# Ordering an mLSTM and mixture-of-depths kernel by hand on one core, with a narrower state product and gates by pairs

## The chip, the cores and the metric

The kernel runs on one core of a Trainium2 chip. The time is the device time of one execution in microseconds (us); the median of several runs is given. The engines are TensorE (PE in the profile; PEld is its loading of weights), VectorE (DVE), ScalarE (ACT), GpSimd (POOL) and SyncE (SP), which only issues transfers here. Each engine works through its own list of instructions in order and waits on semaphores for the others.

## The reference, cut to what matters

There are two blocks. The first is an mLSTM cell over 4 batch rows, 8 heads, 768 tokens and a head size of 40; the second treats its output, 320 wide, as tokens of which the 128 highest scored in each batch row pass a small two-layer network.

```python
for t in range(S):                                   # S = 768, per batch row and head
    m_new  = np.maximum(f_gate[:, :, t] + m, i_gate[:, :, t])
    f_stab = np.exp(f_gate[:, :, t] + m - m_new)
    i_stab = np.exp(i_gate[:, :, t] - m_new)
    m = m_new
    C = f_stab[..., None, None] * C + i_stab[..., None, None] * np.einsum('bhd,bhe->bhde', vt, kt)
    n = f_stab[..., None] * n + i_stab[..., None] * kt
    h_tilde = np.einsum('bhde,bhe->bhd', C, qt)
    denom = np.maximum(np.abs(np.einsum('bhd,bhd->bh', n, qt)[..., None]), 1.0)
    y[:, :, t] = sigmoid(o_gate[:, :, t]) * h_tilde / denom
x = y laid out as (B, S, 320)
scores = np.einsum('bsd,d->bs', x, w_gate)
for b in range(B):
    top = np.argpartition(-scores[b], 128)[:128]
    ye = np.maximum(x[b, top] @ w1, 0.0) @ w2        # 320 -> 1024 -> 320
    out[b, top] = x[b, top] + sigmoid(scores[b, top])[:, None] * ye
```

## The kernel before

The recurrence is done in chunks of 128 tokens: 4 batch rows of 6 chunks are 24 steps. Within a chunk the gates become a matrix W of weights between two tokens, and the state C of all heads is carried from chunk to chunk. One column of ones beside v carries n along with C, so a head has 41 columns, padded to 64 in the state and in the banks of PSUM. All data are 32-bit floats but for the operands of W.

Before a step, a chunk is prepared: W from two small matmuls (pW), an exponential and a causal mask, v scaled by the gates (wv), and k and q transposed (pt to T).

```python
    def prepare(b, c, qk, v1, so):
        W = work.tile([128, H, L], FP, name="W")
        for h0 in range(0, H, 4):
            rows_in = slice(64 * (b % 2) + 8 * h0, 64 * (b % 2) + 8 * h0 + 32)
            pW = ps_t.tile([128, 4, L], FP, name="pW", tag="t")
            nc.tensor.matmul(pW, a_o[b // 2, c][rows_in], M_o[b // 2, c][rows_in], start=True, stop=True)
            nc.scalar.activation(out=W[:, h0:h0 + 4, :], in_=pW, func=AF.Exp)
        nc.gpsimd.affine_select(out=W, in_=W, compare_op=OP.is_ge, fill=0.0, base=0, pattern=[[0, H], [1, L]],
                                channel_multiplier=-1)
        wv = None
        if c < NT - 1:
            wv = work.tile([128, H, D1], FP, name="wv")
            nc.gpsimd.tensor_tensor(out=wv, in0=v1[:, :, 0:D1], op=OP.mult,
                                    in1=cols[c][:, 0, b * H:(b + 1) * H].unsqueeze(2).to_broadcast([128, H, D1]))
        T = work.tile([128, 2, NP, L], FP, name="T")
        for j in range(2):
            pt = ps_t.tile([128, NP, L], FP, name="pt", tag="t")
            for p in range(NP):
                nc.tensor.transpose(pt[:, p, :], qk[:, j, 2 * p:2 * p + 2, :].rearrange("s a d -> s (a d)"), ident)
            nc.scalar.copy(out=T[:, j], in_=pt)
        nc.scalar.activation(out=so, in_=so, func=AF.Tanh, scale=0.5)
        nc.scalar.add(so, so, 1.0)
        return W, T, wv
```

A step then forms the products of q and k (pS), weighs them (P), reads the old state (pI), updates it (pC), adds the part within the chunk (pH) and divides. x is the finished chunk, and its product with w_gate (the reduction into sc) is its score.

```python
    def mlstm_chunk(b, c, qk, v1, so, W, T, wv, x, sc):
        hs = slice(b * H, (b + 1) * H)
        k_n = qk[:, 0]
        P = work.tile([128, NP, 2, L], FP, name="P", bufs=2)
        pS = [ps_s.tile([128, NP, L], FP, name="pS") for _ in range(2)]
        for p in range(NP):
            for j in range(2):
                e = HALVES[j]
                nc.tensor.matmul(pS[j][:, p, :], T[e, 0, p, :], T[e, 1, p, :], start=True, stop=True)
        for j in range(2):
            nc.vector.tensor_tensor(out=P[:, :, j, :], in0=pS[j], op=OP.mult,
                                    in1=W.rearrange("p (n a) t -> p n a t", a=2)[:, :, j, :])
        C = C_t[(b * NT + c) % 3]
        num = None
        if c > 0:
            pI = ps_a.tile([128, H, DP], FP, name="pI", tag="a")
            for p in range(NP):
                for t in HALVES:
                    nc.tensor.matmul(pI[t, 2 * p:2 * p + 2, :].rearrange("t a d -> t (a d)"), T[:, 1, p, t],
                                     C[:, p].rearrange("e a d -> e (a d)"), start=True, stop=True)
            num = work.tile([128, H, D1], FP, name="num")
            nc.vector.tensor_tensor(out=num, in0=pI[:, :, 0:D1], op=OP.mult,
                                    in1=cols[c][:, 1, hs].unsqueeze(2).to_broadcast([128, H, D1]))
        if c < NT - 1:
            pC = ps_a.tile([128, NP, D1], FP, name="pC", tag="a")
            for p in range(NP):
                for j, e in enumerate(HALVES):
                    nc.tensor.matmul(pC[e, p, :], k_n[:, 2 * p + j, :], wv[:, 2 * p + j, :], start=True, stop=True)
            Cn = C_t[(b * NT + c + 1) % 3]
            if c > 0:
                nc.gpsimd.tensor_tensor(out=Cn[:, :, :, 0:D1], in0=C[:, :, :, 0:D1], op=OP.mult,
                                        in1=cols[c][:, 2, hs].rearrange("p (n a) -> p n a", a=2).unsqueeze(3)
                                        .to_broadcast([128, NP, 2, D1]))
            for j in range(2):
                e = slice(j * DP, j * DP + D)
                Cj, pj = Cn[e, :, j, 0:D1], pC[e]
                if c == 0:
                    nc.vector.tensor_copy(out=Cj, in_=pj)
                else:
                    nc.vector.tensor_tensor(out=Cj, in0=Cj, in1=pj, op=OP.add)
        pH = ps_a.tile([128, H, DP], FP, name="pH", tag="a")
        for h in range(H):
            for t in HALVES:
                nc.tensor.matmul(pH[t, h, :], P[:, h // 2, h % 2, t], v1[:, h, :], start=True, stop=True)
        if num is None:
            num = pH
        else:
            nc.vector.tensor_tensor(out=num, in0=num, in1=pH[:, :, 0:D1], op=OP.add)
        den = work.tile([128, H], FP, name="den")
        nc.vector.tensor_scalar(out=den, in0=num[:, :, D], scalar1=-2.0, scalar2=2.0, op0=OP.mult, op1=OP.max)
        nc.vector.scalar_tensor_tensor(out=den, in0=num[:, :, D], scalar=2.0, in1=den, op0=OP.mult, op1=OP.max)
        rec = work.tile([128, H], FP, name="rec")
        nc.vector.reciprocal(out=rec, in_=den)
        sor = work.tile([128, H, D], FP, name="sor")
        nc.gpsimd.tensor_tensor(out=sor, in0=so, in1=rec.unsqueeze(2).to_broadcast([128, H, D]), op=OP.mult)
        nc.vector.tensor_tensor(out=x[:, c, :].rearrange("p (h d) -> p h d", d=D), in0=num[:, :, 0:D], in1=sor,
                                op=OP.mult)
        scr = work.tile([128, DM], FP, name="scr", bufs=1)
        nc.vector.tensor_tensor_reduce(out=scr, in0=x[:, c, :], in1=wg, scale=1.0, scalar=0.0,
                                       op0=OP.mult, op1=OP.add, accum_out=sc[:, c:c + 1])
        nc.gpsimd.dma_start(out=out[b, c * L:(c + 1) * L, :], in_=x[:, c, :])
```

The gates are computed for several chunks at once, in the groups 0, 1 to 2 and 3 to 5. They lie on 128 partitions, four copies of the 32 pairs of batch row and head, so that the three bfloat16 parts of a number (split) can be multiplied in one matmul (operands: a_o and M_o, from which pW is made).

```python
    def gates(c0, c1):
        g, n = slice(c0, c1), c1 - c0
        nc.vector.tensor_tensor_scan(out=flat(F[:, g]), data0=flat(again[:, g]), data1=flat(f_sb[:, g]), initial=0.0,
                                     op0=OP.mult, op1=OP.add)
        nc.vector.tensor_tensor(out=a[:, g], in0=i_sb[:, g], in1=F[:, g], op=OP.subtract)
        nc.vector.tensor_tensor_scan(out=flat(Mg[:, g]), data0=flat(low[:, g]), data1=flat(a[:, g]), initial=0.0,
                                     op0=OP.add, op1=OP.max)
        nc.vector.tensor_tensor_scan(out=m[:, c0 + 1:c1 + 1], data0=Mg[:, g, L - 1], data1=F[:, g, L - 1],
                                     initial=m[:, c0:c0 + 1], op0=OP.max, op1=OP.add)
        mb = m[:, g].unsqueeze(2).to_broadcast([128, n, L])
        nc.vector.tensor_tensor(out=Mg[:, g], in0=Mg[:, g], in1=mb, op=OP.max)
        nc.vector.tensor_tensor(out=wk[:, g], in0=a[0:BH, g], in1=Mg[0:BH, g, L - 1:L].to_broadcast([BH, n, L]),
                                op=OP.subtract)
        nc.scalar.activation(out=wk[:, g], in_=wk[:, g], func=AF.Exp)
        nc.vector.tensor_tensor(out=r[:, g], in0=mb[0:BH], in1=Mg[0:BH, g], op=OP.subtract)
        nc.scalar.activation(out=r[:, g], in_=r[:, g], func=AF.Exp)
        split(M3, Mg, g)
        split(a3, a, g)
        for c in range(c0, c1):
            operands(0, c)
            pc = ps_m.tile([128, 3, BH], FP, name="pc", tag="m")
            for j, row in enumerate((wk[:, c, :], r[:, c, :], r[:, c, L - 1:L].to_broadcast([BH, L]))):
                nc.tensor.transpose(pc[:, j, :], row, ident[0:BH, 0:BH])
            cols.append(const.tile([128, 3, BH], FP, name=f"cols{c}"))
            nc.vector.tensor_copy(out=cols[c], in_=pc)
```

The order of the program is this; a scheduler decides from it how the instructions stand on each engine. The second block's parts are compare (pb spreads a chunk's scores over the partitions, ge and cnt count larger ones), ranks (pcol, sel), gather (pidx, and a transfer of the chosen rows into xe), enter (pX, xeT, the sigmoid), layer1 (ph) and layer2 (py, and a transfer back).

```python
    for n, (b, c) in enumerate(steps):
        for ahead in range(1, AHEAD + 1):
            load(n + ahead)
        if n == 1:
            gates(3, NT)
        if n == 4:
            load_weights()
        if NT <= n < 2 * NT and B > 2:
            operands(1, n - NT)
        if c == NT // 2 and b + 1 < B:
            state[b + 1] = open_batch(b + 1)
        prepared(n + 1)
        mlstm_chunk(b, c, *ready[n], *state[b][0])
        if n > 0:
            compare(*steps[n - 1], *state[steps[n - 1][0]][1])
        if b > 0:
            if c == 1:
                todo = ranks(b - 1, *state[b - 1][1][2:])
            elif c == 2:
                todo = gather(b - 1, todo)
            elif c == 3:
                todo = enter(todo)
                layer1(todo, 0)
            elif c == 4:
                layer1(todo, 1)
            elif c == 5 and b < B - 1:
                layer2(b - 1, todo)
    compare(*steps[-1], *state[B - 1][1])
    picked = gather(B - 1, ranks(B - 1, *state[B - 1][1][2:]))
    if B > 1:
        layer2(B - 2, todo)
    picked = enter(picked)
    for half in range(2):
        layer1(picked, half)
    layer2(B - 1, picked)
```

## Time and profile before

| what | value |
|---|---|
| median of 3 runs | 248.35 us (247.83 to 256.67) |
| span of the profiled run | 250.0 us |
| mean TensorE clock granted in it | 0.914 of full speed |
| transfers | 24.94 MB, 102860 packets, of which 100688 under 512 B |
| queue of the loads (q1) | 16.13 MB, 42.4% of 16 engines' span |
| queue of GpSimd (q0) | 8.03 MB, 10.0% |

A row of the profile's groups gives the line, engine, operation and tiles, the count, the busy time and the mean of one in ns, and the idle time of the engine before it with what ended that. A row of the timeline gives start and duration in us, engine, line, operation, output and inputs, and in brackets the idle time before it. In the rows of 40 slices each digit is a tenth of a slice of 6.25 us; a 9 in the row PEclk stands for 0.9 or more of full speed. Ends of matmuls are modelled, so the distance between starts is the better measure of what a group of matmuls takes.

### The profile page before, as it was taken

To read this page: it belongs to the slowest core of one execution; us is meant where nothing else is said; L and a number is where in the kernel's file an instruction comes from. 1 tells how busy PE (TensorE), PEld (TensorE's weight loads), DVE (VectorE), ACT (ScalarE), POOL (GpSimd) and SP (SyncE) were. 2 spreads that over 40 slices of the span, in tenths; PEclk is the share of its full clock that TensorE was granted. 3 is DMA by queue.
4 is the path that set the end of the run, shared out by engine and by line. 5 is a ranking of instruction groups with operands and counts; after the bars stand their busy time and mean duration, and the time that the engine had idled before them with its cause. 6 is when DMAs were issued, how large, how long until landed. Compare 5 with 4: busy or idle time off the path is not lost. (4 is left out here: it accounts for less than half of the span.)

```text
span 250.0 us, 6255 instructions
## 1 busy us (share of the span) xinstructions
PE 202.1 (81%) x2474; PEld 162.7 (65%) x2474; DVE 166.1 (66%) x450; ACT 89.9 (36%) x199; POOL 110.4 (44%) x148
## 2 busy tenths in 40 slices
PE   0175399999788998699999986999999859927890
PEld 0164268778566786589768774987687749915780
DVE  6479986387888798948637888555478795763100
ACT  1243372255345555332544552523534322100010
POOL 4185651256543757532257575332575633221101
PEclk9998555579999999889999999999999999995998
DMA  4999999539864766573346666563250110000000
GB/s 80 180 156 193 216 283 141 65 61 179 156 116 83 136 124 119 120 131 55 81 105 108 126 116 141 111 113 62 79 108 4 42 41 29 26 29 26 26 0 26
DMA packets 102860, 24.94 MB, mean 100 GB/s; under 512 B 100688, under 2 KB 100944, under 8 KB 102832
## 3 DMA queue, kind: packets, MB, share of 16 engines
q1 hardware_dynamic: 100224, 16.13, 42.4%
q0 software_dynamic: 2224, 8.03, 10.0%
q10 hardware_dynamic: 384, 0.39, 0.8%
q8 instruction: 19, 0.31, 0.5%
q14 instruction: 9, 0.07, 0.1%
HBM read 19.96 MB, written 4.59 MB: 98 GB/s over the span
## 5 line engine op out<-in xcount | busy, mean ns | idle before, releaser
L250 PE MATMUL pS<-T 64*128 64x128 f32 x384 | 40.6, 311 | 0.1
L252 DVE TENSOR_TENSOR P<-pS,W 128x512 f32<-128x512 f32 x48 | 31.4, 681 | 12.8 <-PE pS L250 12.7
L250 PEld LDWEIGHTS pS<-T 64*128 64x128 f32 x384 | 31.5, 202 | 9.4 <-issue 7.2
L289 PE MATMUL pH<-v,P 128*64 128x64 f32 x768 | 31.5, 234 | 6.3 <-DVE P L252 3.1
L221 ACT ACTIVATE W<-pW 128x512 f32<-128x512 f32 x48 | 26.9, 596 | 24.8 <-PE pW L220 24.5
L222 POOL TENSOR_SCALAR_AFFINE_SELECT W<-W 128x1024 f32<-128x1024 f32 x24 | 28.2, 1175 | 17.1 <-ACT W L221 16.9
L289 PEld LDWEIGHTS pH<-v,P 128*64 128x64 f32 x768 | 27.0, 145 | 12.4 <-DVE num L264 6.1
L233 PE MATMUL pt<-ident,qk 128*128 128x128 f32 x192 | 32.4, 312 | 3.0 <-ACT W L221 2.7
L302 POOL TENSOR_TENSOR sor<-so,rec 128x320 f32<-128x320 f32 x24 | 17.6, 731 | 32.0 <-DVE rec L300 31.9
L234 ACT COPY T<-pt 128x512 f32<-128x512 f32 x48 | 26.6, 587 | 11.7 <-PE pt L233 11.5
L233 PEld LDWEIGHTS pt<-ident,qk 128*128 128x128 f32 x192 | 24.1, 158 | 7.5 <-ACT W L221 4.8
L227 POOL TENSOR_TENSOR wv<-v,cols 128x328 f32<-128x328 f32 x20 | 15.3, 763 | 31.2 <-PE pC L272 8.5
L386 PE MATMUL ph<-xeT,w 128*128 128x128 f32 x192 | 23.8, 279 | 0.8 <-DVE xeT L375 0.8
L261 PE MATMUL pI<-C,T 128*64 128x128 f32 x320 | 24.3, 290 | 0.0
L386 PEld LDWEIGHTS ph<-xeT,w 128*128 128x128 f32 x192 | 22.3, 192 | 1.6 <-DVE xeT L375 1.0
L316 ACT COPY sb<-pb 128x128 f32<-128x128 f32 x24 | 6.4, 266 | 45.9 <-PE pb L315 45.9
L308 POOL DMA_DIRECT2D out_dram<-x x24 | 14.1, 589 | 18.1 <-DVE x L303 16.5
L303 DVE TENSOR_TENSOR x<-num,sor 128x320 f32<-128x320 f32 x20 | 9.8, 492 | 18.4 <-POOL sor L302 18.4
L275 POOL TENSOR_TENSOR C<-C,cols 128x328 f32<-128x328 f32 x16 | 16.1, 1008 | 12.5 <-DVE C L284 10.4
L394 PE MATMUL py<-w,hT 128*128 128x320 f32 x64 | 20.6, 475 | 0.0
L261 PEld LDWEIGHTS pI<-C,T 128*64 128x64 f32 x320 | 18.6, 142 | 2.9 <-issue 0.6
L318 DVE SCALAR_TENSOR_TENSOR ge<-sb,sc,earlier 128x128 bf16<-128x128 f32 (+5 forms) x24 | 16.9, 704 | 1.9 <-ACT sb L316 1.3
(107 smaller groups left out, 275.7 us busy)
## 6 DMA issues: line engine op xcount, KB each, us to landing
qk<-in_k_dram SPq DMA_DIRECT2D x24, 160.0 KB, 3.5
qk<-in_q_dram SPq DMA_DIRECT2D x24, 160.0 KB, 3.7
v<-in_v_dram SPq DMA_DIRECT2D x24, 160.0 KB, 3.0
so<-in_o_gate_dram SPq DMA_DIRECT2D x24, 160.0 KB, 2.9
out_dram<-x POOLq DMA_DIRECT2D x24, 160.0 KB, 2.6
w<-in_moe_w_dram POOLq DMA_DIRECT2D x1, 1280.0 KB, 7.9
w<-in_moe_w_dram POOLq DMA_DIRECT2D x2, 512.0 KB, 8.1
i_sb<-in_i_gate_dram ACTq DMA_DIRECT2D x4, 80.0 KB, 6.1
```

Source lines behind the costliest of these rows:

```text
L221: nc.scalar.activation(out=W[:, h0:h0 + 4, :], in_=pW, func=AF.Exp)
L222: nc.gpsimd.affine_select(out=W, in_=W, compare_op=OP.is_ge, fill=0.0, base=0, pattern=[[0, H], [1, L]], channel_multiplier=-1)
L233: nc.tensor.transpose(pt[:, p, :], qk[:, j, 2 * p:2 * p + 2, :].rearrange("s a d -> s (a d)"), ident)
L234: nc.scalar.copy(out=T[:, j], in_=pt)
L250: nc.tensor.matmul(pS[j][:, p, :], T[e, 0, p, :], T[e, 1, p, :], start=True, stop=True)
L252: nc.vector.tensor_tensor(out=P[:, :, j, :], in0=pS[j], op=OP.mult, in1=W.rearrange("p (n a) t -> p n a t", a=2)[:, :, j, :])
L261: nc.tensor.matmul(pI[t, 2 * p:2 * p + 2, :].rearrange("t a d -> t (a d)"), T[:, 1, p, t], C[:, p].rearrange("e a d -> e (a d)"), start=Tr ...
L289: nc.tensor.matmul(pH[t, h, :], P[:, h // 2, h % 2, t], v1[:, h, :], start=True, stop=True)
L302: nc.gpsimd.tensor_tensor(out=sor, in0=so, in1=rec.unsqueeze(2).to_broadcast([128, H, D]), op=OP.mult)
L318: nc.vector.scalar_tensor_tensor(out=ge[:, GE[u]:GE[u + 1]], in0=sb.rearrange("p t l -> p (t l)")[:, 0:n], scalar=sc[:, u:u + 1], in1=earl ...
L386: nc.tensor.matmul(ph[:, f, :], w1[:, j, (f0 + f) * 128:(f0 + f + 1) * 128], xeT[:, j, :], start=(j == 0), stop=(j == NDC - 1))
L394: nc.tensor.matmul(py, hT[:, f, :], w2[:, f, :], start=(f == 0), stop=(f == NFC - 1))
```

## The change

The scheduler is switched off and the order on every engine is written by hand, step by step. Each of the following goes with it.

- T, W and wv are made two steps ahead; pb and the comparison take the scores of the step before; ph and py are spread over the steps in pieces, and in the last stretch py stands between the comparison and the gather.
- pI and pC share one bank of PSUM (pIC) and are not padded: the state has 41 columns a head, so pI streams 82 columns for two heads instead of 128.
- The causal mask is applied to each half of W as soon as its exponential is done.
- The stores of x and the loads of w1, w2 and w_gate are issued by SP, the loads' queue, instead of GpSimd.
- The gates are computed in the groups 0, 1, 2 to 3 and 4 to 5, on 32 partitions. The three parts of a number are now three tiles, and the operands come from six accumulated matmuls instead of two; the two exponentials of the gates are done chunk by chunk with the subtraction as their bias. Parts of the splitting go to ACT and GpSimd.
- Four chunks instead of three are loaded ahead.

The diff, cut to its core:

```diff
-    C_t = [const.tile([128, NP, 2, DP], FP, name=f"C{n}") for n in range(3)]
+    C_t = [const.tile([128, NP, 2, D1], FP, name=f"C{n}") for n in range(3)]
...
+        for x, xs, cast, sub in zip((Mg, a), parts, (nc.scalar.copy, nc.gpsimd.tensor_copy), (nc.vector, nc.gpsimd)):
+            if c0 == 0:
+                cast, sub = nc.vector.tensor_copy, nc.vector
+            rest = gate.tile([BH, 2, L], FP, name="rest", bufs=2)
+            cast(out=xs[0][:, g], in_=x[:, g])
+            sub.tensor_tensor(out=rest[:, 0:n], in0=x[:, g], in1=xs[0][:, g], op=OP.subtract)
+            cast(out=xs[1][:, g], in_=rest[:, 0:n])
+            sub.tensor_tensor(out=xs[2][:, g], in0=rest[:, 0:n], in1=xs[1][:, g], op=OP.subtract)
+    def scales(c):
+        nc.scalar.activation(out=wk[:, c], in_=a[:, c], func=AF.Exp, bias=nM[:, c:c + 1], scale=1.0)
+        nc.scalar.activation(out=r[:, c], in_=Mg[:, c], func=AF.Exp, bias=m[:, c:c + 1], scale=-1.0)
...
+        pO = ps_m.tile([128, 2, L], FP, name="pO", tag="m")
+        for j in range(2):
+            for part in range(3):
+                nc.tensor.matmul(pO[:, j, :], place[j][u][:, part].rearrange("p g k h -> p (g k h)"),
+                                 parts[j][part][:, c, :], start=(part == 0), stop=(part == 2))
+        M_o[u, c] = const.tile([128, 4, L], BF, name=f"M_o{u}{c}")
+        a_o[u, c] = const.tile([128, L], BF, name=f"a_o{u}{c}")
+        nc.scalar.activation(out=a_o[u, c], in_=pO[:, 1, :], func=AF.Identity, bias=of[:, 0:1], scale=1.0)
+        nc.vector.scalar_tensor_tensor(out=M_o[u, c], in0=pO[:, 0, :].unsqueeze(1).to_broadcast([128, 4, L]),
+                                       scalar=of[:, 1:2], in1=which.unsqueeze(2).to_broadcast([128, 4, L]),
+                                       op0=OP.add, op1=OP.mult)
...
-        nc.gpsimd.dma_start(out=w2, in_=moe_w2.rearrange("(f p) d -> p f d", p=128))
...
+            nc.sync.dma_start(out=w1[0:w, j, :], in_=moe_w1[d0:d0 + w, :])
+        nc.sync.dma_start(out=w2, in_=moe_w2.rearrange("(f p) d -> p f d", p=128))
...
-        nc.gpsimd.affine_select(out=W, in_=W, compare_op=OP.is_ge, fill=0.0, base=0, pattern=[[0, H], [1, L]],
-                                channel_multiplier=-1)
...
+            nc.gpsimd.affine_select(out=W[:, h0:h0 + 4, :], in_=W[:, h0:h0 + 4, :], compare_op=OP.is_ge, fill=0.0, base=0,
+                                    pattern=[[0, 4], [1, L]], channel_multiplier=-1)
...
+    def exchange(b, c, qk, T, wv):
+        pIC = ps_c.tile([128, (H + NP) * D1], FP, name="pIC")
+        pI, pC = pIC[:, 0:H * D1], pIC[:, H * D1:].rearrange("p (n d) -> p n d", d=D1)
+        if c > 0:
+            C = C_t[(b * NT + c) % 3]
+            for p in range(NP):
+                for t in HALVES:
+                    nc.tensor.matmul(pI[t, 2 * p * D1:2 * (p + 1) * D1], T[:, 1, p, t],
+                                     C[:, p].rearrange("e a d -> e (a d)"), start=True, stop=True)
...
-            pI = ps_a.tile([128, H, DP], FP, name="pI", tag="a")
-            for p in range(NP):
-                for t in HALVES:
-                    nc.tensor.matmul(pI[t, 2 * p:2 * p + 2, :].rearrange("t a d -> t (a d)"), T[:, 1, p, t],
-                                     C[:, p].rearrange("e a d -> e (a d)"), start=True, stop=True)
...
-        pH = ps_a.tile([128, H, DP], FP, name="pH", tag="a")
-        for h in range(H):
-            for t in HALVES:
-                nc.tensor.matmul(pH[t, h, :], P[:, h // 2, h % 2, t], v1[:, h, :], start=True, stop=True)
...
+        pH = ps_h.tile([128, H, DP], FP, name="pH")
+        for j in range(2):
+            for p in range(NP):
+                for t in HALVES:
+                    nc.tensor.matmul(pH[t, 2 * p + j, :], P[:, p, j, t], v1[:, 2 * p + j, :], start=True, stop=True)
...
+        nc.sync.dma_start(out=out[b, c * L:(c + 1) * L, :], in_=x)
...
-        nc.gpsimd.dma_start(out=out[b, c * L:(c + 1) * L, :], in_=x[:, c, :])
...
+    def weighed(n):
+        W[n] = weigh(*steps[n])
+        wv[n] = scaled_v(*steps[n], loaded[n][1])
+    def first_weighed(n):
+        c = steps[n][1]
+        operands(0, c)
+        W[n] = weigh(*steps[n])
+        scales(c)
+        columns(c)
+        wv[n] = scaled_v(*steps[n], loaded[n][1])
+    def step(n):
+        b, c = steps[n]
...
+        load(n + AHEAD)
+        decay(b, c)
+        P = scores(W[n], T[n])
+        if NT <= n + 2 < N:
+            weighed(n + 2)
+        num = exchange(b, c, qk, T[n], wv[n])
+        if n == 0:
+            turned(1)
+            first_weighed(1)
+            gated(1)
+        pH = within(P, v1)
         if n > 0:
...
+            pb, pc = steps[n - 1]
+            spread(pc, *state[pb][1][:2])
+        if b > 0 and c == 1:
+            pcol = columns_of(state[b - 1][1][2])
+        if b > 0 and c == 2:
+            picked[b - 1] = gather(b - 1, sel[b - 1])
+        if b > 0 and c == 3:
+            layers[b - 1] = Layers(b - 1, *picked[b - 1])
+        num, sor = norm(num, pH, so)
+        if n > 0:
+            compare(pc, *state[pb][1])
+        if n + 2 < N:
+            if n + 2 < NB:
+                pad(nc.gpsimd, n + 2)
+            turned(n + 2)
+            gated(n + 2)
+        result(b, c, num, sor, state[b][0])
+        if b > 1 and c < 2:
+            layers[b - 2].second(c * NFC // 2, (c + 1) * NFC // 2)
         if b > 0:
...
+                sel[b - 1] = ranks(pcol, state[b - 1][1][3])
...
+                layers[b - 1].gate()
+                layers[b - 1].first(0, 2)
+            elif c > 3:
+                layers[b - 1].first(3 * c - 10, 3 * c - 7)
+        if n + 2 < NT:
+            if n % 2 == 0:
+                gates(n + 2, n + 4)
+            first_weighed(n + 2)
+        if 4 <= n < 4 + NT:
+            operands(1, n - 4)
+    load(0)
+    nc.sync.dma_start(out=wg, in_=_bcast(moe_w_gate, 128))
+    gates(0, 1)
...
+    operands(0, 0)
+    turn(loaded[0][0], 1, T[0])
+    W[0] = weigh(0, 0)
+    scales(0)
+    gated(0)
+    columns(0)
+    wv[0] = scaled_v(0, 0, loaded[0][1])
+    load(1)
+    pad(nc.gpsimd, 1)
+    gates(1, 2)
+    load(2)
+    load(3)
+    for n in range(N):
+        step(n)
...
```

In the last stretch the order is pb and the comparison, py for half of the hidden columns, pcol, sel, py for the other half, pidx, the gather, pX and the rest.

## The prediction

> **What bounds the kernel now.** I read the page's busy shares and slices first, then the times of the 24 stores of x (one per step, a step being one chunk of 128 tokens of one batch row), then the timeline of two steps in the middle and of the end.
>
> ```profile
> PE 202.1 (81%) x2474; PEld 162.7 (65%) x2474; DVE 166.1 (66%) x450; ACT 89.9 (36%) x199; POOL 110.4 (44%) x148
> ...
> PE   0175399999788998699999986999999859927890
> ...
> PEclk9998555579999999889999999999999999995998
> ```
>
> PE is the fullest engine, and its clock is halved from slice 4 to slice 8. The stores show where the time lies:
>
> ```profile
> 32.28 0.58 POOL L308 DMA_DIRECT2D out_dram<-x  x1
> 55.45 0.58 POOL L308 DMA_DIRECT2D out_dram<-x  x1
> ...
> 73.39 0.58 POOL L308 DMA_DIRECT2D out_dram<-x  x1 [0.82 <-DVE x L303]
> 80.54 0.58 POOL L308 DMA_DIRECT2D out_dram<-x  x1 [0.82 <-DVE x L303]
> ...
> 222.27 0.58 POOL L308 DMA_DIRECT2D out_dram<-x  x1 [0.82 <-DVE x L303]
> ```
>
> So there are three stretches: a ramp of 80.5 us for the six steps of batch row 0, 18 even steps of (222.27-80.54)/18 = 7.87 us, and a tail of 27.7 us. In the even steps the starts on the timeline give what PE spends per group with its clock up:
>
> ```profile
> 99.36 1.09 PE L261 MATMUL pI<-C,T 128*64 128x128 f32 x16
> 100.28 0.62 PE L272 MATMUL pC<-wv,qk 128*64 128x41 f32 x16
> 100.45 0.49 DVE L303 TENSOR_TENSOR x<-num,sor 128x320 f32<-128x320 f32 x1 [1.08 <-POOL sor L302]
> ...
> 101.46 1.53 DVE L306 CUSTOM_DVE_ANT_0 scr<-x,wg 128x320 f32<-128x320 f32 x1
> 101.88 0.76 POOL L227 TENSOR_TENSOR wv<-v,cols 128x328 f32<-128x328 f32 x1
> ...
> 103.06 0.32 PE L315 MATMUL pb<-ident,sc 128*128 128x128 f32 x1 [2.16 <-DVE sc L306]
> ```
>
> pI takes 100.28-99.36 = 0.92, and by the same reading pS 1.08, pC 0.55, pH 1.08, pt 1.03, the pW pair 0.32, pb 0.15. pI exists in 5 of 6 steps and so does pC: 1.08+0.77+0.46+1.08+1.03+0.32+0.15 = 4.9 us. The second block adds per batch row ph 5.36, py 4.27, pcol, pX and pidx 1.4: 11 us, 1.8 a step. Against 6.7 needed, 7.87 are spent: PE loses 15% to waits such as the last line's, where pb waits for sc in front of ready work. In the tail an order hurts too:
>
> ```profile
> 226.51 6.67 PE L394 MATMUL py<-w,hT 128*128 128x320 f32 x16
> ...
> 230.13 0.49 DVE L365 CUSTOM_DVE_ANT_0 scre<-xe,wg 128x320 f32<-128x320 f32 x1 [3.28 <-DMA xe<-out_dram,idx]
> ...
> 233.01 0.49 PE L373 MATMUL pX<-ident,xe 128*128 128x128 f32 x3
> ```
>
> The gathered rows are there at 230.1, but pX stands behind py until 233.0.
>
> **What the Trainium skill says.** "TensorE: Matmul & The Clock Gate", Part 1, says that the clock starts at half, is released after about 3.4 us of activity, and falls back after an idle window. The trace agrees in part: after 2.16 us without matmuls before 103.06 the clock is 0.5 from 104 to 108, then 1.0. But from 36 to 53 PE is full and the clock stays 0.5; the page's trace caveats name such a stuck state. The same page, Part 2, says that matmuls keep program order; pX behind py is that. "SBUF — State Buffer", Who interferes with whom, says that a VectorE instruction with two SBUF inputs contends with a GpSimd one that reads SBUF: the score reduction L306 takes 0.49 alone and 1.53 beside wv above. "DMA: Bandwidth & Descriptors", Issuing engines are not separate DMA queues, says that changing the issuing engine saves only its issue time: here 24 x 0.589 = 14.1 us of POOL, no transfer.
>
> **The change, part by part.**
>
> *Narrow state read.* pI streams 82 columns instead of 128: 0.92 x 82/128 = 0.59, just above the 16 x 34 ns that pC and pH show as their spacing. It saves 0.33 us in each of 20 steps, 6.6 us of PE, all of it where PE is the bound.
>
> *Even steps by hand.* The new order on PE is pS(n), pW(n+2), pI, pC, pH, pb(n-1), pt(n+2), a piece of the second block. T, W and wv are made two steps ahead, pb asks for scores one step old, and pH starts on the first half of P. PE needs 4.6 + 1.8 = 6.4. VectorE, counted from the end of pS: P twice 1.4, num 0.5, C twice 0.65, num+pH 0.5, den and rec 0.6, and then sor on GpSimd, x 0.5, reduction 0.57. The comparison ge (0.35 to 1.02, two SBUF inputs) is placed just where sor runs; I take it that one shuts out the other, so 0.7 + 0.75 instead of the larger. Then comes decay, also on GpSimd, beside x and the reduction: 0.5 more. Sum about 6.2 to 6.6, plus 1.4 in the step with sel and 1.2 in the one with the gate. So the two engines are nearly level. Taking the longer one step by step, with PE's py halves in c=0 and 1 and ph in 3, 4 and 5, I get 6.5, 7.8, 6.6, 7.7, 7.0, 6.5 = 42.1 a batch row, 7.0 a step; row 1 has no py, but six small matmuls and M_o (0.68 on VectorE) for the operands in four steps, and comes to about 44. With the three rows at 42.1, 42.1 and 44, 128 us for 18 steps against 141.7: -13.5.
>
> *Ramp.* Less is loaded first: the gates go in once instead of four times (192 KB instead of 768 KB), 32 partitions in place of 128, and three issues on the ACT queue instead of eight. I put v of chunk 0 at 8 us instead of 11.6, the first M_o at 7.8 (13.3 before), P(0) at 15, after the gates of chunk 1 which stand ahead of it on VectorE, and x(0) at 25 (29.6 before). But then the order has a serial stretch: in steps 0 to 3 the operands of n+2 come at the end of step n, and pS(n+1) stands behind pW(n+2) and pc(n+2). From pS: 1.08, then pI, pC and pH 2.25, num and den 1.15, sor 0.85, x and reduction 1.1, M_o 0.85, pW 0.3, two exps 1.2, two short exps 0.6, pc 0.35: 9.7 us with the clock up. With the clock at half pS, pI, pC, pH and pc add 3.3: 13. In steps 0 and 2 the pair's gates come before M_o: scan 0.62, subtraction 0.42, scan 0.67, 0.2, 0.35, 0.15 and the split with its hops to ACT 1.5, near 4 us, PE standing still. So pS(1) at 33, then 11.5, 15.5 and 11.5 (middle between the clocks) put pS(4) at 71.5, x(4) at 79 and x(5) at 85.5, against 73.4 and 80.5. Here the change costs about 5, between -2 and +12 with the clock.
>
> *Masks in halves, stores on SP.* Two affine_selects replace one of 1175 ns; nobody waits for their sum, since W is two steps ahead. The stores take 14 us off GpSimd, which is not the bound; sor gets through sooner.
>
> *Tail.* py is put into the waits for ge and sel, so that pX can start with the data: up to 3.0 gained. But py's first half runs at half clock (4.2 us of 0.53 each), delays pcol by some 2 and pidx by 1, and PE then idles in the gather, so that part of ph runs slow. I count +0.5.
>
> Sum: 85.5 + 128 + 28.2 = 241.7 of span. The profiled span was 250.0 for a median of 248.35, so 1.65 less: 240.
>
> **Rivals.** (1) The ramp's serial chain is worse than I think: if the clock is stuck at half up to step 4 as it was up to 53 us here, x(5) comes at 92, and with even steps of 7.3 the total is 250: no gain. For it: the ramp's gaps of 1.5 to 2.5 us between PE groups. Against it: the clock stays at 1.0 between 65 and 75 although PE is busy in 7 of 10 us only. (2) VectorE becomes the bound: if every two-input instruction is shut out in turn by GpSimd, c=1 and c=3 become 8.5 and the others 7.3, 46 a row, 138 in all: 250 again. (3) The hand order gives PE all it needs: 6.6 a step and a warm ramp, x(5) at 78, 119 for the steps, a tail of 26: 221. Against it stands the VectorE sum above. (4) The loads bind: 4.4 us of DMA per chunk (42.4% of 250 us over 24 chunks) against 7 us steps leave room, and the weights, now on the load queue, delay chunk 8, which is wanted two steps later. I give this little.
>
> **Range and chances.** The ramp is uncertain by 7 us, the even steps by 8, the tail by 2; together some 10 us at 8 in 10, a little less below since VectorE sets a floor. So 240, from 228 to 251. 2% below is 243.4, 2% above 253.3: faster 0.60, within 0.27, slower 0.13.
>
> **What would show it.** Stores of x at about 25, 86 and 214 us; even steps near 7.0 to 7.2; pI's spacing near 37 ns; PE idle before pW in steps 0 to 3 put down to M_o or to W's exps, 2 to 8 us each; reduction and x longer than 0.5 beside decay; pX right after the gather. I am wrong if the ramp ends before 78 (the chain overlaps more than I read from the order), if even steps pass 7.5, or if loads appear as what matmuls wait for.

## The result and the profile after

The changed kernel takes 255.64 us (median of 4 runs, 255.36 to 256.67) against 248.27 for the kernel before: the ratio is 1.031, 95% interval 1.027 to 1.035. It is slower; 240 was predicted. The kernel before scatters from run to run more than most of the others (245.7 to 256.8 over all comparisons), so intervals of ratios are wide, and for the four kernels of one comparison none is given; what follows rests on the stretches of the profiles. Times are medians of all runs, ratios compare only the runs within 1.5% of the fastest of their kernel, and some profiles are of slower runs: that of the kernel before took 252.58 us, 4.3 more than its median (that of the changed kernel took 255.36), and those of 6 and 16 below took 261.08 and 250.01, where the runs compared took 254.3 to 256.2 and 245.3 to 248.2. Where the 4.3 us lie in the stretches below is not known.

By the stores of x, as in the prediction:

| stretch, us | before | predicted | after |
|---|---|---|---|
| ramp, to the store of x(5) | 80.5 | 85.5 | 94.5 |
| 18 even steps | 141.7 | 128 | 126.5 |
| tail | 27.7 | 28.2 | 32.5 |
| span of the profile | 250.0 | 241.7 | 253.6 |

So the even steps won what was expected (as much as 4.3 us of it may be that excess of the profiled run), and the ramp and the tail lost 14.0 and 4.8. The page of the changed kernel, busy shares and slices (6.34 us each):

```profile
PE 191.0 (75%) x2522; PEld 160.6 (63%) x2522; DVE 154.7 (61%) x429; ACT 97.7 (39%) x218; POOL 104.5 (41%) x162
...
PE   1775366473576988977999999499999988780991
...
PEclk9995557575586899998899999889999999997598
```

TensorE is now 11 us less busy and yet the kernel is longer: the 6th to the 13th slice have it at 3 to 7 tenths, where the kernel before had 7 to 9. That is the ramp, from 32 to 82 us. One cycle of it on the timeline of the changed kernel (start, duration, engine, line, operation; in brackets the idle time before it and what ended that):

```profile
35.00 2.08 PE L269 MATMUL pS<-T 64*128 64x128 f32 x16
...
41.99 0.72 POOL L334 TENSOR_TENSOR sor<-so,rec 128x320 f32<-128x320 f32 x1 [4.06 <-DVE rec L332]
...
42.66 0.41 POOL L105 MEMSET qk<- 128x384 f32 x1
...
43.12 1.40 PE L229 MATMUL pt<-ident,qk 128*128 128x128 f32 x8 [2.15 <-POOL qk L105]
...
45.04 0.47 ACT L240 ACTIVATE so<-so 128x320 f32<-128x320 f32 x1
...
45.92 0.35 ACT L196 ACTIVATE a_o<-pO,of 128x128 bf16<-128x128 f32 x1
46.31 0.75 DVE L197 SCALAR_TENSOR_TENSOR M_o<-pO,of,which 128x512 bf16<-128x512 f32 x1 [2.53 <-ACT a_o L196]
47.11 0.61 PE L249 MATMUL pW<-M_o,a_o 32*128 32x512 bf16 x2 [1.84 <-DVE M_o L197]
...
49.20 0.31 PE L206 MATMUL pc<-ident,wk 32*128 32x32 f32 x1 [1.49 <-ACT wk L183]
...
49.84 2.08 PE L269 MATMUL pS<-T 64*128 64x128 f32 x16
```

pS of the next step comes at 49.84, directly behind pc: 14.8 us after the pS before it at 35.00. Every engine waits for another in turn: the transposes for a padding that GpSimd writes behind sor, VectorE for a_o, which stands on ScalarE behind the copies of those transposes and the two operations on so (the output gate), TensorE for M_o and then for wk. The waits of the changed kernel between 25 and 86 us (total, times, longest):

```profile
PE pW L249 <- DVE M_o L197: 6.9, 4, 2.6
PE pt L229 <- POOL qk L105: 6.4, 3, 2.4
...
PE pc L206 <- ACT wk L183: 5.9, 4, 1.5
...
PE pO L192 <- ACT M L177: 4.3, 2, 2.1
```

In the even steps two lines of the costliest groups show the price of the new order (count, then total and mean ns):

```profile
L334 POOL TENSOR_TENSOR sor<-so,rec 128x320 f32<-128x320 f32 x24 | 24.1, 1005 | 45.9 <-DVE rec L332 42.9
...
L339 DVE TENSOR_TENSOR x<-num,sor 128x320 f32<-128x320 f32 x20 | 14.0, 702 | 14.1 <-POOL sor L334 14.1
```

sor took 731 and x 492 before. One step, the third of batch row 2, took 11.2 us instead of some 7 (single steps are counted from one end of x to the next); its timeline:

```profile
151.78 1.04 POOL L431 DMA_INDIRECT out_dram<-ye,idx  x1 [3.03 <-DVE rank L373]
...
155.13 0.16 DVE L384 TENSOR_SCALAR idx<-pidx 128x1 uint32<-128x1 f32 x1 [0.18 <-PE pidx L382]
...
157.05 1.07 POOL L386 DMA_INDIRECT xe<-out_dram,idx  x1 [1.58 <-DVE ge L355]
...
158.16 0.73 POOL L334 TENSOR_TENSOR sor<-so,rec 128x320 f32<-128x320 f32 x1
```

The gather's index is there at 155.3, but the gather goes out at 157.05, and sor, ready at about 156.5, stands behind it. The bracket names ge, which is no input of the gather; what the gather does need is the scatter of the row before, whose landing took 4.5 us this time (median 2.5). It landed at 156.25, and the gather followed 0.8 us later, as in the tail. The code says why: gather and scatter each name all rows of out from the first up to their own batch row as one region, so the two regions overlap. The tail shows the same wait by its name:

```profile
227.44 0.15 DVE L384 TENSOR_SCALAR idx<-pidx 128x1 uint32<-128x1 f32 x1
227.80 1.03 POOL L431 DMA_INDIRECT out_dram<-ye,idx  x1 [7.29 <-DVE idx L384]
231.14 1.03 POOL L386 DMA_INDIRECT xe<-out_dram,idx  x1 [2.31 <-DMA out_dram<-ye,idx]
234.22 0.87 PE L398 MATMUL pX<-ident,xe 128*128 128x128 f32 x3 [7.16 <-DMA xe<-out_dram,idx]
235.66 8.51 PE L417 MATMUL ph<-xeT,w 128*128 128x128 f32 x48 [0.57 <-ACT xeT L400]
```

Scatter first, gather 3.5 us behind the index, and then ph at half pace, 8.51 us for what takes 5.6 at full pace.

### The profile page after: what moved, and what is told of

The parts are those of the page before. It is cut to its first block, busy times and chain, and to the rows that moved or that the text cites. A ratio compares the mean times of both kernels' runs of the same rounds, so it can differ in the third digit from the quotient of the medians.

```text
span 253.6 us, 6331 instructions
## 1 busy us (share of the span) xinstructions
PE 191.0 (75%) x2522; PEld 160.6 (63%) x2522; DVE 154.7 (61%) x429; ACT 97.7 (39%) x218; POOL 104.5 (41%) x162
## 4 chain that ended last, share of the span: by engine, by line
PE 35%; DVE 13%; issue 11%; POOL 5%; DMA 3%; POOLq 1%; ACT 0%; DVEq 0%
PE pH L319 9%; PE pS L269 5%; PE ph L417 5%; PE pt L229 4%; POOL sor L334 4%; PE py L426 3%; DVE x L339 3%; PE pIC L291 3%; DVE scr L342 2%; DVE P L271 2%; DMA out_dram<-ye,idx 2%; PE pIC L297 2%; PE pb L348 2%; DVE num L326 1%; PE pW L249 1%
## 5 line engine op out<-in xcount | busy, mean ns | idle before, releaser
L251 POOL TENSOR_SCALAR_AFFINE_SELECT W<-W 128x512 f32<-128x512 f32 x48 | 31.0, 669 | 54.4 <-ACT W L250 54.4
L334 POOL TENSOR_TENSOR sor<-so,rec 128x320 f32<-128x320 f32 x24 | 24.1, 1005 | 45.9 <-DVE rec L332 42.9
L229 PEld LDWEIGHTS pt<-ident,qk 128*128 128x128 f32 x192 | 25.7, 162 | 12.7 <-POOL qk L105 6.9
L269 PE MATMUL pS<-T 64*128 64x128 f32 x384 | 32.5, 316 | 0.0
L269 PEld LDWEIGHTS pS<-T 64*128 64x128 f32 x384 | 27.4, 216 | 3.9 <-issue 2.1
L417 PEld LDWEIGHTS ph<-xeT,w 128*128 128x128 f32 x192 | 26.3, 221 | 1.0 <-ACT xeT L400 1.0
L339 DVE TENSOR_TENSOR x<-num,sor 128x320 f32<-128x320 f32 x20 | 14.0, 702 | 14.1 <-POOL sor L334 14.1
L291 PE MATMUL pIC<-C,T 128*64 128x82 f32 x320 | 18.0, 262 | 0.0
L291 PEld LDWEIGHTS pIC<-C,T 128*64 128x64 f32 x320 | 14.5, 154 | 4.5 <-issue 3.4
L249 PE MATMUL pW<-M_o,a_o 32*128 32x512 bf16 x48 | 10.9, 427 | 8.4 <-DVE M_o L197 8.4
L431 POOL DMA_INDIRECT out_dram<-ye,idx x4 | 4.1, 1025 | 30.5 <-DVE ye L429 17.2
```

What stands on the lines that cost most here:

```text
L251: nc.gpsimd.affine_select(out=W[:, h0:h0 + 4, :], in_=W[:, h0:h0 + 4, :], compare_op=OP.is_ge, fill=0.0, base=0, pattern=[[0, 4], [1, L]], ...
L291: nc.tensor.matmul(pI[t, 2 * p * D1:2 * (p + 1) * D1], T[:, 1, p, t], C[:, p].rearrange("e a d -> e (a d)"), start=True, stop=True)
L339: nc.vector.tensor_tensor(out=x.rearrange("p (h d) -> p h d", d=D), in0=num[:, :, 0:D], in1=sor, op=OP.mult)
L417: nc.tensor.matmul(self.ph[:, f % 4, :], w1[:, j, f * 128:(f + 1) * 128], self.xeT[:, j, :], start=(j == 0), stop=(j == NDC - 1))
```

## The experiments

Stretches from here on go by the start of x itself on VectorE, about 0.5 us before its store: in some of the faster kernels a few stores queue behind the weights. Where nothing in a stretch was changed, it repeats to 1 or 2 us (ramp 94.0 to 94.9, tail 31.5 to 33.3, steps 125.9 to 126.7 and twice 128.4).

| kernel | ramp | steps | tail | span | time | ratio, interval |
|---|---|---|---|---|---|---|
| before | 79.8 | 141.7 | 28.5 | 250.0 | 248.27 | 1 |
| changed | 94.0 | 126.5 | 33.1 | 253.6 | 255.64 | 1.031 (1.027-1.035) |
| 1 gather ahead of scatter | 94.9 | 126.7 | 27.7 | 249.3 | 251.70 | 1.017 (1.007-1.026) |
| 2 and py behind the gather | 94.0 | 128.4 | 27.0 | 249.4 | 250.26 | 1.009 (1.005-1.012) |
| 3 sor ahead of the gather | 94.7 | 121.8 | 32.1 | 248.6 | 250.25 | 1.012 (0.998-1.027) |
| 4 paddings early | 92.2 | 126.7 | 31.5 | 250.4 | 252.32 | 1.020 (1.007-1.032) |
| 5 ramp reordered | 84.1 | 125.9 | 32.6 | 242.6 | 247.66 | 0.992 (0.986-0.997) |
| 6 before, narrow state | 83.7 | 144.9 | 29.6 | 258.2 | 257.69 | 1.030 (1.018-1.042) |
| 7 one mask, stores on GpSimd | 93.9 | 124.2 | 33.3 | 251.3 | 252.77 | 1.019 (1.009-1.029) |
| 8 parts 2 to 5 together | 85.1 | 122.3 | 27.1 | 234.5 | 235.75 | 0.953 (0.943-0.962) |
| 9 and a second ramp order | 69.8 | 120.0 | 27.1 | 216.9 | 218.55 | - |
| 10 stores alone on GpSimd | 93.6 | 125.1 | 32.8 | 251.5 | 253.19 | - |
| 11 padded state, pC beside pH | 103.1 | 146.1 | 32.6 | 281.7 | 287.31 | - |
| 12 as 9, stores on GpSimd | 71.6 | 127.6 | 27.5 | 226.7 | 227.93 | - |
| 13 long streams of pI | 98.6 | 125.6 | 32.1 | 256.3 | 257.97 | 1.037 (1.018-1.055) |
| 14 ge behind the reduction | 95.6 | 130.1 | 31.8 | 257.5 | 259.69 | 1.046 (1.029-1.063) |
| 15 as 9, long streams of pI | 69.4 | 121.4 | 25.4 | 216.2 | 219.11 | 0.882 (0.853-0.911) |
| 16 TensorE kept busy in the ramp | 88.2 | 128.4 | 31.6 | 248.3 | 251.55 | 0.994 (0.987-1.002) |
| 17 as 9, and in the tail | 69.8 | 120.1 | 25.7 | 215.7 | 219.11 | 0.877 (0.867-0.888) |

### The tail: 1 and 2

```diff
-    layers[B - 2].second(NFC // 2, NFC)            # py's second half, ye, scatter
-    last = Layers(B - 1, *gather(B - 1, sel))
+    layers[B - 2].second(NFC // 2, NFC, close=False)
+    found = gather(B - 1, sel)
+    layers[B - 2].close()                          # 1: ye and scatter behind the gather
+    last = Layers(B - 1, *found)
```

In 2 the whole of `second` follows `gather`.

> The last gather is asked for before the scatter of batch row 2 instead of behind it; nothing else moves. Theory: in the changed kernel the gather waited 2.31 us for that scatter to land, because both name overlapping rows of out as a whole, and the issue of the scatter stood ahead of it too (index ready at 227.6 us, gather issued at 231.1). Then the gather goes out within 0.5 us of the index and the tail falls from 32.5 us to about 29.3 (-3.2); total near 252.5. Rival: the gather is slow by itself[...] and the order is not what costs: tail 32 or more, total unchanged at 255.6.

> The gather before the scatter as in the run before, and also the second half of py moved from before the index matmuls to behind them, so that TensorE works on it while the gather is under way. Theory: py's second half (2.1 us) leaves the path to the gather, TensorE is kept busy, and ph (48 matmuls) takes about 5.6 us as in the kernel before instead of 8.5: tail 32.5 to about 26, total near 249. Rival: the clock falls during sel (no matmul for 2 us) and stays at half anyway: ph still 8.5 us, the tail about 28.5, total near 251.5.

The tail fell by 5.4 and 6.1 us. The timeline of 1:

```profile
228.15 0.16 DVE L384 TENSOR_SCALAR idx<-pidx 128x1 uint32<-128x1 f32 x1 [1.24 <-PE pidx L382]
228.59 1.05 POOL L386 DMA_INDIRECT xe<-out_dram,idx  x1 [7.02 <-DVE idx L384]
...
231.71 0.52 PE L398 MATMUL pX<-ident,xe 128*128 128x128 f32 x3 [3.59 <-DMA xe<-out_dram,idx]
...
232.79 7.11 PE L417 MATMUL ph<-xeT,w 128*128 128x128 f32 x48 [0.57 <-ACT xeT L400]
```

The gather follows the index by 0.44 us. It goes out 7.0 us after x(23) instead of 10.6; that is 3.6 of the 5.4, and most of the rest is ph, 7.11 instead of 8.51. So standing behind the scatter is the cause, and the rival (a gather slow by itself) falls: from its issue to its landing it took 3.0 us here and 2.9 before. Moving py (2) gave only 0.7 more: ph took 7.25 there, not 5.6, since TensorE still stands still before pX.

### The gather in the even steps: 3

```diff
-        if b > 0 and c == 2:                       # ahead of norm(): gather, then sor on GpSimd
-            picked[b - 1] = gather(b - 1, sel[b - 1])
         num, sor = norm(num, pH, so)
+        if b > 0 and c == 2:
+            picked[b - 1] = gather(b - 1, sel[b - 1])
```

> In the steps that gather (c=2 of rows 1 to 3) the gather is issued behind sor on GpSimd instead of ahead of it, and its index behind the denominators on VectorE. Theory: the 8.4, 11.2 and about 9 us steps are long because sor stands behind the gather (issue 1.07 us, and 4 us more at the second one, where the gather waits for the scatter of the row before). Then they come to about 7.0, 7.3 and 7.0: -7 in all, total near 248.5. Rival: GpSimd is only held up later, in decay and the masks of the next step, and the wait for the scatter is passed on: -2, total near 253.5.

-4.7 us: the three steps took 7.4, 8.4 and 8.4 instead of 8.4, 11.2 and 9.2, and part was handed on: two steps behind the second of them a step took 9.2 instead of 7.5, since TensorE waited 1.50 us for the gathered rows and ran slowly behind that (pt 1.91 us, for 1.04 one step later). That lies between the two theories.

### The ramp: 4, 5, 8 and 9

4 writes the paddings of chunks 2 to 4 before the first step. 5 changes the order in steps 1 to 4:

```diff
         P = scores(W[n], T[n])
+        if 1 <= n < NT - 1:
+            operands(0, n + 1)                     # pO, a_o, M_o: one step ahead, not two
         num = exchange(b, c, qk, T[n], wv[n])
+        if 1 <= n < NT - 1:
+            first_weighed(n + 1)                   # pW, exps, masks, wk, pc, wv
...
             if n % 2 == 0:
                 gates(n + 2, n + 4)
-            first_weighed(n + 2)                   # with operands(0, n + 2)
```

> The paddings of chunks 2 to 4 are written before the first step instead of behind sor in steps 0 to 2. Theory: the transposes pt(n+2) waited 2.4, 2.2 and 1.9 us for them in the ramp, and with them the copies of T and a_o on ScalarE, which M_o stands behind: the ramp (store of x of step 5, 94.5 us) ends 3 to 6 us earlier, total near 251. Rival: the chain gates, M_o, pW, masks sets the ramp and hides the paddings: under 1 us.

> Only the first five steps are reordered: the small matmuls pO of chunk n+1 stand behind pS(n), its weights pW, scales and columns behind pI and pC of step n (in place of: all of chunk n+2 at the end of step n, in front of pS(n+1)); the gates of the pairs stay at the end of steps 0 and 2, but TensorE no longer waits for them there. Theory: the ramp is long because pS(n+1) stands behind a chain over five engines (gates, M_o, pW, exponentials, columns). Then x(5) comes near 74 us: 25 for x(0), five steps of some 7.3, 5.2 us for each pair of gates and about 2 for row transposes and paddings; the even steps and the tail keep their 126.5 and 32 us, total near 235. Rival A: the gates themselves (VectorE, with casts on ScalarE and GpSimd) set the pace: x(5) at 85 or more, total 246. Rival B: the half clock: unchanged, since the two profiles with the ramp at full and at half clock end it at 95.4 and 94.5 us this is already unlikely.

4 gave 1.8 to 2.7 us of the 6.4 us of waits it removed: the chain behind hid the rest. 5 gave 9.9 (ramp 84.1), where rival A's line was 85: the chain in front of pS was a cause, but the gates still stood on VectorE in front of P(1) and P(3), TensorE waiting behind pO for them, and wk still stood behind the exponentials of W, with pH waiting behind pc. TensorE's pace had changed only in part there (pS 2.08, 1.87 and 2.08 us in steps 1 to 3).

> The ramp reordered, the paddings ahead of the first step, the gather behind sor, and the last gather ahead of py's second half and of the scatter, together. If the stretches are independent: ramp near 72 us, steps 121.8 as measured with the gather moved, tail 26.5: span near 220, time 222 (ratio 0.89 to 0.90 against the kernel before). If the faster ramp only moves a wait (chunks not yet loaded, weights of the second block late, VectorE full): 232 or more.

8 joined 2, 3, 4 and 5. The stretches add up as measured one by one (85.1, 122.3, 27.1); only the 72 us that I had put in for the ramp was wrong, as in 5.

9 then changed the ramp again:

```diff
+        if 1 <= n < NT - 1:
+            scales(n + 1)                          # wk, r ahead of a_o and the exps of W
+            operands(0, n + 1)
...
+        if n in (1, 2):
+            gates(n + 3, n + 4)                    # chunk 4 in step 1, chunk 5 in step 2
...                                                 # step 0: gates(2, 4) ahead of pH(0)'s denominators
```

> As the combination before, with the ramp's order changed once more: the gates of chunks 2 and 3 stand in step 0 ahead of its denominators (VectorE idled there for 4.7 us), those of chunks 4 and 5 one by one behind the state update of steps 1 and 2; and wk and r are made before the exponentials of W on ScalarE, so that pc doesn't wait for them (1.5 to 2 us in each step). Theory: what was left of the ramp was the 5.2 us of gates in front of P(1) and P(3), with TensorE behind pO, and the wait for wk in front of pH: steps of about 7.5, x(5) at 66 to 70 instead of 85.6, total 235.75 less 16 to 20, near 218. Rival: the chunks' loads or the state chain hold the ramp: x(5) at 80 or later, total 230 or more.

The ramp took 69.8 us and the kernel 218.55, both as expected. The page of 9:

```profile
PE 180.1 (83%) x2522; PEld 151.2 (70%) x2522; DVE 154.3 (71%) x437; ACT 96.5 (44%) x220; POOL 105.8 (49%) x166
...
PE   0798967686698796989999997999999999956990
```

The instructions are those of the changed kernel but for eight more on VectorE and a few elsewhere. What cost 24 us in the ramp was the order, the place of the paddings included, and the slow TensorE that came of it: in 9 pS takes 1.37 and 1.94 us in steps 1 and 2 and 1.16 from step 3 on, where the changed kernel has 2.08 in steps 1 to 4. The two moves in 9 (gates; wk with pc ahead of pW) were not tried apart. This kernel beats both: 17, which is 9 but for 8 filler matmuls, has the ratio 0.877 (0.867 to 0.888) to the kernel before.

### The pace of TensorE: 16 and 17

The half clock was my first rival. The granted clock can't settle it, as two profiles of the same ramp show; windows of the changed kernel and of kernel 1 (stretch, us; busy of PE, PEld, VectorE, ScalarE, GpSimd; granted clock, DMA share, GB/s), with pS of kernel 1 in that stretch:

```profile
25.00:44.00 19.00, 10.87 (x107) 8.89 (x106) 10.22 (x26) 5.28 (x13) 7.53 (x13) 0.59 0.36 51
```

```profile
25.00:44.00 19.00, 10.65 (x101) 8.63 (x102) 10.22 (x25) 5.09 (x12) 7.89 (x15) 1.00 0.35 51
...
35.53 2.08 PE L269 MATMUL pS<-T 64*128 64x128 f32 x16
```

The row says 0.59 and 1.00, and yet TensorE is equally busy, and pS takes 2.08 us in both, where an even step has 1.16. (In what I expected of 5 I argued from this row that the clock is out; that was no argument.) So TensorE was kept busy instead, with `warm(k)`, k matmuls of the identity with itself that nobody reads:

```diff
+        if n in (2, 4):
+            warm(8)
         operands(0, c)
+        warm(5)
         W[n] = weigh(*steps[n])
         scales(c)
+        warm(6)
         columns(c)
```

> Of the changed kernel, only this: TensorE's waits in the preparation of chunks 1 to 5 (for the gates, M_o and wk) are filled with 11 to 19 matmuls on a constant, whose result nobody reads, 0.13 us each at full pace and 0.25 at half. Theory A, the half pace costs: pS, pI, pC, pH and pc take 3.3 us more in a step than at full pace; kept busy, pS returns to 1.16 us, the four cycles shorten by 2 to 3 us each, and x(5) comes at 83 to 87 instead of 94, total near 246. Theory B, the chain over the other engines sets the ramp and TensorE's pace is hidden or can't be raised this way: x(5) at 93 to 97.

The timeline of 16, the third group of fillers in the first cycle (each filler leaves two records) and what follows it:

```profile
32.65 1.94 PE L461 MATMUL warm<-ident 128*128 128x128 f32 x12
34.51 0.24 PE L206 MATMUL pc<-ident,wk 32*128 32x32 f32 x1
34.60 0.28 PE L206 MATMUL pc<-ident,F 32*128 32x32 f32 x2
34.81 1.16 PE L269 MATMUL pS<-T 64*128 64x128 f32 x16
35.90 0.79 PE L291 MATMUL pIC<-C,T 128*64 128x82 f32 x16
```

pS is back at 1.16, pI at 0.79 (1.36 before), and the ramp falls to 88.2: the half pace, which follows from the waits, costs about 6 of the 94 us, less than theory A asked. By the starts of x, 1.0 of it comes before x(0), and the four cycles shorten by 1.2, 0.8, 0.6 and 2.1 us, not by 2 to 3 each. The Trainium skill, "TensorE: Matmul & The Clock Gate", Part 1, says that activity releases the clock and an idle window takes it back; this run agrees in the pace of the matmuls. It is the smaller part, and not to be added to the 24 us of 9, which contain a good part of the same return to full pace.

> The fastest kernel, with 8 matmuls on a constant between py's second half and pX, in the 1.3 us in which TensorE waits for the gathered rows. Theory: ph takes 7.25 us there instead of 5.6 because TensorE paused; kept busy it takes about 5.7: tail 27.1 to 25.6, total 217. Rival: the pause of 0.6 us behind pX slows it anyway: unchanged, 218.5.

In 17 ph takes 5.62 us and the tail 25.7 instead of 27.1; the rival falls. The time is 219.11 against 218.55: a gain of 1.4 is inside the scatter of a few runs.

### The narrow state read: 6, 11, 13 and 15

> The kernel before with one part of the change alone: the state without padding (41 columns instead of 64), so that pI streams 82 columns. Theory of the prediction: TensorE bounds the steps, pI falls from 0.92 to 0.59 us in 20 steps: -4 to -6.6, ratio 0.975 to 0.985. Rival: in the kernel before the steps are set by waits (sor on GpSimd, scores on VectorE) and the narrow read only makes a wait longer: under -1.5, ratio 0.994 to 1.0.

6 (in the kernel before, C and pI allocated with 41 columns instead of 64, nothing else written differently) came out 3% slower, outside both theories. It is no test: the kernel before is ordered by its scheduler, which put the matmuls of TensorE into another order; in its profile x(0) came already 6.4 us late.

> Of the changed kernel, only the state padded to 64 columns again, so that pI streams 128 columns; pI has a bank to itself and pC lies beside pH. Theory of the prediction: pI's 16 matmuls take 0.92 us instead of 0.63, all of it on the path where TensorE is the bound: 20 x 0.3 = +6. Rival: in the hand order VectorE and GpSimd set the steps and pI runs beside P: +0 to +2; even steps 126.5 to 128.5.

11 (C and pI padded again, pC moved into one tile with pH, whose streams are cut from 64 to 41 columns so that both fit) was 31.7 us slower than the changed kernel, also outside both. Its waits between 103 and 250 us:

```profile
PE pHC L323 <- DVE C L313: 16.4, 12, 3.2
...
PE pHC L323 <- DVE C L311: 4.6, 3, 2.5
```

pH waits for the state update that reads pC from the same tile. So this measures the sharing and not the width; whether the wait is in the bank or only in the tracking of tiles wasn't tried. 13 changes only the length of the streams:

```diff
-                    nc.tensor.matmul(pI[t, 2 * p * D1:2 * (p + 1) * D1], T[:, 1, p, t],
-                                     C[:, p].rearrange("e a d -> e (a d)"), start=True, stop=True)
+                    nc.tensor.matmul(pIC[t, 2 * p * D1:2 * p * D1 + 128], T[:, 1, p, t],
+                                     C[:, 2 * p * D1:2 * p * D1 + 128], start=True, stop=True)
```

> Of the changed kernel, only the length of pI's streams: each of its 16 matmuls a step reads 128 columns again instead of 82 (the 46 surplus ones run over the next pair's columns and are overwritten by the next matmul; bank, layout and order stay). Theory of the prediction: all of it lies where TensorE is the bound: 20 x 0.3 = +6, even steps 126.5 to 131 or more. Rival: pI runs beside P on VectorE, and VectorE with GpSimd sets the steps: under +2.

> The same lengthening of pI's streams in the fastest kernel so far (218.55 us, TensorE busy 83%). Theory: there TensorE has less room, so that 20 x 0.3 = 6 us come back in full: 224 or more. Rival: VectorE sets its steps too: 220 or less.

The group of pI in 13:

```profile
L294 PE MATMUL pIC<-C,T 128*64 128x128 f32 x320 | 25.4, 308 | 0.0
```

TensorE works 7.4 us more (18.0 before the edit), and the even steps take 125.6 us instead of 126.5: no loss in the sum. The ramp, where pI stands in the chain, grew by some 4 us; the whole by 2.3, within the intervals. In 15 the even steps grew by 1.4 and the time by 0.6. The rival's forecast holds in both: most of the 6.6 us of TensorE's work lay off the path.

The 0 of 13 is two effects, though. In the four steps with py it lost 0.2 to 0.3 us each (1.1 in all, and as much in 15); two others, the fifth of rows 1 and 2, were 0.7 and 0.9 us shorter, since TensorE kept its pace over a wait that slowed it in the changed kernel. The transposes behind that wait in row 2, in the changed kernel and in 13:

```profile
164.13 1.91 PE L229 MATMUL pt<-ident,qk 128*128 128x128 f32 x8
...
167.80 1.04 PE L232 MATMUL pt<-ident,qk 128*128 128x128 f32 x8
```

Whether the longer streams kept the pace up was not tried apart. What the narrow read is worth in the even steps is thus about 1 to 1.4 us, not 0.

### Comparison, masks and stores: 14, 7, 10 and 12

> Of the changed kernel, only the comparison ge of the step before moved on VectorE from between the denominators and x to behind the score reduction. Theory of the prediction: ge and sor shut each other out, so sor comes earlier by as much as ge takes (sor back to about 0.72 us, from 1.0 on average) and ge then stands alone: the even steps stay within 1.5 us of 126.5. Rival: they really overlap: each step grows by ge's 0.35 to 1.02 us, 18 x 0.7 = +12.

The group of sor in 14 (ge placed after the score reduction):

```profile
L334 POOL TENSOR_TENSOR sor<-so,rec 128x320 f32<-128x320 f32 x24 | 17.4, 723 | 50.8 <-DVE rec L332 50.7
```

sor is back from 1005 to 723 ns, so ge does hold it up; in the changed kernel sor grows from 0.72 to 1.39 us as ge grows from 0.30 to 1.02. But the steps took 130.1, +3.6 (1.7 above the longest unchanged ones): neither 0 nor 12. ge starts 0.15 to 0.2 us ahead of sor, and that head start, the hop from rec to GpSimd, was free; 18 x 0.2 = 3.6 is of this size. But by single steps the change runs from -0.8 to +0.9 us, so that this is what was lost is not shown. They exclude each other for most of ge, not for all.

> Of the changed kernel, the mask in one piece again and the stores of x issued by GpSimd again; nothing else. Theory of the prediction: GpSimd is not the bound and nobody waits for the mask: 255.6 within 1. Rival: a store's 0.58 us of issue on GpSimd stands in front of decay and the masks in each step, and sor comes later by as much: +5 to +10.

> Of the changed kernel, only the stores of x on GpSimd again; masks stay in halves. With both undone the even steps took 124.1 instead of 126.5 us, and the step with the second gather 8.7 instead of 11.2. Theory: a store on the load queue holds the next chunk's loads back until x is there (they were issued at 149.8 to 152.6), and they then run beside the scatter, which the gather waits for; so the stores alone give the gain: even steps 124, that step near 9, total 252.5 to 253.5. Rival: it is the mask (one instruction instead of two on GpSimd): then this run stays at 126.5 and 255.6.

With both undone the even steps took 124.2, with the stores alone 125.1: the stores on the load queue may have cost some 1.4 to 2.3 us there, but unchanged steps reach down to 125.9, so the sum is hardly clear of the spread between runs. Clear is the step with the second gather, 8.7 and 8.8 us instead of 11.2. The loads of a chunk now stand behind a store that waits for x (issued 149.8 to 152.6), beside the scatter, which landed in 4.5 us; in 7 and 10 its slowest landing is 2.6. The loads need not be the reason: in 9 a scatter of the tail, with no chunk left to load, landed in 4.5 as well. And a store on GpSimd stood between sor and decay, so that x came ahead of decay: x takes 492 ns in all 20 steps, not 702 on average.

> The run with the ramp's second order and, besides, the stores of x on GpSimd. If the stores matter only through the loads beside the scatter, and the gather already stands behind sor: within 1.5 us of that run, either way. If 0.58 us of issue in front of decay and the masks binds: +5 or more.

In the better order the same move cost 9.4 us: the even steps took 127.6 instead of 120.0. One reason is on the timeline of 10, where it happened too:

```profile
106.19 0.58 POOL L340 DMA_DIRECT2D out_dram<-x  x1 [0.82 <-DVE x L339]
...
106.35 3.09 DVE L372 TENSOR_TENSOR rank<-cnt,later 128x6 f32<-128x6 f32 x1
106.80 0.75 POOL L279 TENSOR_TENSOR C<-C,cols 128x328 f32<-128x328 f32 x1
107.49 1.22 POOL L251 TENSOR_SCALAR_AFFINE_SELECT W<-W 128x512 f32<-128x512 f32 x2
108.68 0.73 POOL L259 TENSOR_TENSOR wv<-v,cols 128x328 f32<-128x328 f32 x1
```

An addition of six columns, 0.16 us in the changed kernel, ends at 109.44 with GpSimd's wv: it seems to have been held through five GpSimd instructions. In 12 it took 2.39, ending with the second mask and ahead of wv, and that step 10.3 us instead of 7.4; in 7 it took 1.23, ending with decay (C). The rest of the 9.4 was not traced.

## Why the prediction was wrong, by its own steps

The span was predicted at 241.7 and came at 253.6: +9.0 in the ramp, -1.5 in the even steps, +4.3 in the tail. The 1.65 us that I took off the span set the span of the profiled run beside the median of others; that run itself took 252.58 for its 250.0, and the changed kernel 255.36 for 253.6. By these the time is 1.8 to 2.6 us above the span, so that a span of 241.7 meant about 244.

*Ramp (the step that failed most).* The mechanism was named rightly: x(0) at 25 (24.8 measured), then "pS(n+1) stands behind pW(n+2) and pc(n+2)". The cycle was mis-sized: 11.5, 15.5 and 11.5 predicted, 14.8, 18.2 and 11.4 measured, pS(1) at 35.0 for 33, and x(4) at 88.5 for 79. The term that failed is the one between sor and M_o: I counted 1.1 us there, for x and the reduction, and in the cycle shown it is 3.6 (42.71 to 46.31). On that path stand the padding behind sor, the transposes, and on ScalarE the copies of T, the operations on so and a_o; none of them is in my sum. The padding alone was worth 1.8 to 2.7 us in the whole ramp (4). The gates took 5.2 us from F to the last part in step 0, for "near 4". And the half pace I had put at the middle between the clocks; pS took 2.08 us, the half pace, in all four cycles. (The page's clock was at half in slices 5 to 8, not "from slice 4".) Rival 1 foresaw the length (x(5) at 92), but named the pace alone for it: 16 shows 6 us, where 9, which changes the order and with it the pace, gains 24.

*Even steps.* The sum was right, 7.03 us a step for 7.0, the parts were not. "6.6 us of PE, all of it where PE is the bound" is wrong: by 13 and 15 it is about 1 to 1.4. What gained the rest of the 15.2 us must then be the order itself; that is by elimination, no run undid it, and the 4.3 us that the profiled run before took above its median may be part of it. Row 2 went 5.9, 6.7, 11.2, 6.3, 7.5, 6.5 against the predicted 6.5, 7.8, 6.6, 7.7, 7.0, 6.5: the steps with sel and with the gate were over-counted by 1.1 and 1.4, and the gather in front of sor (1.07 us of issue, and a wait for the scatter) was left out; 3 takes 4.7 us away. That ge and sor shut each other out holds but for the start of ge (14). Decay beside x was to cost 0.5 in every step; x was that much longer in six of 20 steps, 1.1 us longer in one and not at all in the others: 0.2 on average.

*Masks and stores.* I counted them as nothing; undoing both gained 2.3 us in the even steps, hardly more than the spread between runs. That the stores' 14 us on GpSimd are off the path fits 7 and 10, but not 12, where putting them back cost 9.4. That the queue of the stores has an order of its own was overlooked.

*Tail.* +0.5 predicted, +4.8 measured. py did take its place in the waits, but "pX right after the gather" assumed a gather that follows its index; it followed the scatter (3.6 us by 1). ph at half pace, of which I had expected only a part to be slow, cost 2.9.

*What would have shown it.* Of my three conditions (ramp under 78, steps over 7.5, loads) none came true: the first guarded against the wrong side, and none against a longer ramp.

## What to carry to other kernels

When an order is fixed by hand, write down for the first steps, too, what each engine's next instruction waits for: the ramp here lost 24 us through its order and the slow TensorE that followed from it. Test a shorter matmul stream by lengthening it in the finished kernel, with the order held fixed, before crediting it, and see that TensorE's pace stays the same; here some 7 us of TensorE's work were worth 1 to 1.4. And put an indirect gather ahead of a scatter that names an overlapping region, or its wait for the landing becomes part of the path.

## What the runs showed of the hardware that was not expected

- A VectorE addition of 128 x 6 with two inputs in SBUF took 3.09 us in 10, from its start during GpSimd's store issue to the end of the fifth of five back-to-back GpSimd instructions, and 0.16 where GpSimd paused. The Trainium skill, "SBUF — State Buffer", Who interferes with whom, says that a VectorE instruction with two SBUF inputs contends with a GpSimd one that reads SBUF; here it waited for up to five of them, and in 12 (2.39 us) for four. That this is the contention of the page is argued; no run tests it.
- The granted clock of the profile does not show TensorE's half pace: at 1.00, pS took 2.08 us as at 0.59, and 1.16 behind three groups of filler matmuls (6.3 us of the 10 us before it).
- A scatter of 128 rows landed in 2.5 us most times, in 4.5 beside four chunk loads of 160 KB, and in 9 once in 4.5 with no chunk load under way; what makes it slow stays open.
